# Loading chunk 0's K and Q in halves of heads, with another order of the opening, in a fused window-attention and maxout kernel

## The chip, the cores and the metric

The kernel runs on one core of a Trainium2 chip. The metric is the time of one execution in device microseconds (us). PE is the matrix engine (PEld its weight loads), DVE the vector engine, ACT the scalar engine, POOL the GpSimd engine; SP issues DMAs. Inputs and output are float32; the kernel works in bfloat16 on the chip and sums in float32.

## The reference

A sliding-window attention with four sink tokens (4 batches, 8 heads, 768 tokens, head size 64) feeds a feed-forward layer that takes the maximum of three products:

```python
    scores = scale * np.matmul(q, k.transpose(0, 1, 3, 2))
    keep = is_sink | in_window          # position < 4, or 0 <= i - j < 128
    scores = np.where(keep, scores, -1000000000.0)
    a = np.exp(scores - np.max(scores, axis=-1, keepdims=True))
    a = a / (np.sum(a, axis=-1, keepdims=True) + 1e-09)
    x = np.matmul(a, v)                 # then (B*S, H*D) = (3072, 512)
    h = np.maximum(np.maximum(x @ w1, x @ w2), x @ w3)   # 512 -> 768
    out = h @ w_out                                      # 768 -> 512
```

## The kernel before

The 3072 tokens are cut into 12 chunks of 256, three per batch. A window of 128 tokens needs at most the last half of the chunk ahead, and the four sinks come from the batch's first chunk. For each chunk (number `ci` in the calls) the work is this:

- `load` (line 90): K, Q and V of all 8 heads, 512 KB each, by DMA from SP's queue into one of two slots per kind. With `parts` a load can be cut into groups of heads. A `gate` is a tiny write by POOL into the slot, for which the DMA then waits; `after(wi)` (490) makes the gate wait for a piece of weights.
- `cast_qk` (102) and `cast_v` (108) cast to bfloat16, on the engine named in the call; a call takes half of the heads, or a quarter of V.
- `turn` (118) and `turn2` (140) turn half of K's or Q's heads by four PE transposes through PSUM and copy them to `kT` or `qT`. From chunk 4 on, a DMA does it (`turn_dma`, 157 and 162).
- `score` (287) makes the scores of a head pair, `premask` (269) puts an additive mask into PSUM ahead of it, `expo` (335) takes exponentials on ACT, `mask` (341) multiplies masks in on DVE for pairs without `premask`.
- `sink_k`, `sink_score` and `sink_v` (242, 349, 365) handle the sinks. `av_open` and `av` (381, 398) multiply with V on PE; DVE normalises by a reciprocal (403) and a product (406) into `x_sb`.
- `xpose` (419) turns x into `xT` for the feed-forward layer, by PE and a copy (420); from chunk 4 on a DMA does it.
- `ffn_h(ci, fp, wi)` (438): eight matmuls of 128x256 for columns 256 fp to 256 fp + 255 of weight matrix `wi` (0 to 2). For `wi` 0 ACT copies the result to `h_sb` (445); for 1 and 2 DVE takes the maximum with what stands there (449). So the two maxima of a group of columns read ACT's copy.
- `ffn_y` (459, copies at 461): the output product with `wo`, six matmuls of 128x512; `store` sends it out.

The weights come by DMA from POOL's queue (`load_w` 251, `load_wo` 257), cast on the way, in pieces of 256 or 512 columns. `masks_late` (213, 215) makes multiplicative masks on POOL; `masks_packed` (221 to 224) makes four more copies of them on ACT, for the packed scores of chunks 6 and 9 (`score_packed`). `warm` (180) issues products of zeros that fill PE's time at the start.

Nothing reorders the work: each engine runs its instructions in the order in which the calls stand in the program. PSUM has 8 banks, handed out in the order in which earlier tiles are given back in the program, so a call also waits for its bank's last reader. The opening, lines 507 to 709 before, is one flat list of calls, up to chunk 3's `xpose`. From line 715 a loop runs chunks 3 to 11 by fixed patterns.

Of the kernel before, what the change touches and what calls it, by code (L numbers as in the profile page):

```python
# [16 lines left out]
def kernel(  # L17
# [13 lines left out]
    nc = tc.nc  # L31
# [17 lines left out]
    with tc.manual_schedule():  # L49
# [26 lines left out]
        def load(ci, what="kqv", gate=None, part=None, parts=1):  # L76
            if ci >= NCH:
                return
            b, c = divmod(ci, CPB)
            t0 = c * 256  # L80
            for w in what:
                src = {"k": k, "q": q, "v": v}[w]
                if (ci, w) not in raws:
                    raws[ci, w] = raw.tile([128, H, 2, D], F32, tag=w + "_raw", name=w + "_raw")
                dst = raws[ci, w]
                if gate is not None:
                    gate(dst[0:1, 0, 0, 0:1])
                n = H // parts
                for g in range(parts) if part is None else (part,):
                    nc.sync.dma_start(  # L90
                        out=dst[:, n * g:n * g + n],
                        in_=src[b, n * g:n * g + n, t0:t0 + 256]
                            .rearrange("h (p i) d -> p h (i d)", i=2))

        def cast_qk(ci, w, g, eng):
            if ci >= NCH:
                return
            if (ci, w) not in bfs:
                bfs[ci, w] = raw.tile([128, NP, 2, 2, D], BF16, tag=w + "_bf", name=w + "_bf")
            x, y = bfs[ci, w], raws[ci, w]  # L100
            f = eng.copy if eng is nc.scalar else eng.tensor_copy
            f(x[:, 2 * g:2 * g + 2].rearrange("q p i a d -> q p a i d"),  # L102
              y[:, 4 * g:4 * g + 4].rearrange("q (p a) i d -> q p a i d", a=2))
# [409 lines left out]
        premask(0, (0,))  # L513
        warm(9)
        cast_qk(0, 'k', 0, nc.scalar)
        turn(0, 'k', 0, nc.vector)
        load(0, 'v')
        cast_qk(0, 'q', 0, nc.scalar)
        turn(0, 'q', 1, nc.vector)
        sink_init()  # L520
        warm(1)
        cast_qk(0, 'k', 1, nc.gpsimd)
        cast_v(0, 1, 0, nc.vector)
        turn(0, 'k', 1, nc.scalar)
        load(1, 'k')
        turn(0, 'q', 0, nc.scalar)
        cast_v(0, 0, 1, nc.vector)
        score(0, (2,))
        masks_late()
        premask(0, (1,))  # L530
        load_w(0, 512, 768)
        load_w(0, 0, 512)
        cast_v(0, 0, 0, nc.vector)
        load(1, 'q')
        score(0, (0,))
        sink_k(0)
        expo(0, 2)
        load_w(1, 512, 768)
        cast_qk(1, 'k', 0, nc.vector)
        expo(0, 0)  # L540
        premask(0, (3,))
        cast_v(0, 1, 1, nc.vector)
        cast_qk(1, 'q', 0, nc.gpsimd)
        score(0, (1,))
        premask(1, (1,))
        turn2(1, 'k', 0, nc.vector)
        cast_qk(1, 'k', 1, nc.scalar)
        score(0, (3,))
        expo(0, 1)
        cast_qk(1, 'q', 1, nc.gpsimd)  # L550
        load(1, 'v')
        turn2(1, 'k', 1, nc.scalar)
        expo(0, 3)
        av_open(0)
        av(0, 0)
        av(0, 1)
        sink_v(0)
        turn2(1, 'q', 0, nc.vector)
        load_w(1, 0, 512)
        turn2(1, 'q', 1, nc.scalar)  # L560
        av(0, 2)
        av(0, 3)
        cast_v(1, 1, 1, nc.vector)
        score(1, (0,))
        expo(1, 0)
        sink_score(1)
        cast_v(1, 0, 1, nc.gpsimd)
        score(1, (1,))
        cast_v(1, 1, 0, nc.gpsimd)
        load(2, 'q', gate=pool_gate)  # L570
        score(1, (2,))
        expo(1, 2)
        xpose(0, 1, nc.vector)
        xpose(0, 0, nc.vector)
        cast_v(1, 0, 0, nc.vector)
        premask(1, (3,))
        expo(1, 1)
        score(1, (3,))
        ffn_h(0, 2, 0)
        mask(1, 2)  # L580
        load(2, 'k', gate=after(0, 300))
        mask(1, 0)
        load_w(2, 512, 768)
        av_open(1)
        av(1, 2)
        av(1, 1)
        load_w(2, 0, 256)
        expo(1, 3)
        load(2, 'v', gate=after(1))
        av(1, 0)  # L590
        ffn_h(0, 1, 0)
        load(3, 'q', gate=after(0))
        av(1, 3)
        ffn_h(0, 0, 0)
        load_w(2, 256, 512)
        xpose(1, 1, nc.vector)
        xpose(1, 0, nc.scalar)
        ffn_h(0, 2, 1)
        cast_qk(2, 'q', 0, nc.gpsimd)
        load_wo(0, 3)  # L600
        ffn_h(1, 0, 0)
        ffn_h(1, 1, 0)
        load_wo(3, 6)
        ffn_h(1, 2, 0)
        load(3, 'k', gate=after(1))
# [5 lines left out]
        load(3, 'v', gate=after(2))  # L611
        cast_qk(2, 'k', 1, nc.scalar)
        cast_qk(2, 'k', 0, nc.gpsimd)
        cast_qk(2, 'q', 1, nc.vector)
        ffn_h(1, 2, 1)
        turn(2, 'q', 0, nc.scalar)
        ffn_h(1, 2, 2)
        turn(2, 'q', 1, nc.scalar)
        turn(2, 'k', 1, nc.vector)
        cast_v(2, 0, 1, nc.gpsimd)  # L620
        turn(2, 'k', 0, nc.vector)
        ffn_h(1, 0, 2)
        load(4, 'q')
        sink_score(2)
        score(2, (1,))
        load(4, 'k', gate=after(2))
        cast_v(2, 0, 0, nc.gpsimd)
        score(2, (2,))
        score(2, (3,))
        expo(2, 3)  # L630
        expo(2, 1)
        ffn_h(1, 1, 2)
        ffn_h(0, 0, 2)
        expo(2, 2)
        mask(2, 1)
        ffn_h(0, 1, 2)
        cast_v(2, 1, 1, nc.vector)
        cast_qk(3, 'q', 0, nc.gpsimd)
        cast_v(2, 1, 0, nc.vector)
        score(2, (0,))  # L640
        mask(2, 2)
        expo(2, 0)
        mask(2, 0)
        av_open(2)
        mask(2, 3)
        cast_qk(3, 'q', 1, nc.gpsimd)
        load(4, 'v', gate=pool_gate)
        ffn_y(1, 0)
        ffn_y(0, 0)
        cast_qk(3, 'k', 0, nc.scalar)  # L650
        av(2, 2)
        ffn_y(0, 1, nc.vector)
        av(2, 0)
        turn(3, 'q', 1, nc.scalar)
        turn(3, 'q', 0, nc.scalar)
        av(2, 3)
        av(2, 1)
        cast_qk(3, 'k', 1, nc.scalar)
        turn(3, 'k', 0, nc.scalar)
        cast_v(3, 1, 0, nc.vector)  # L660
        ffn_y(1, 1)
        cast_v(3, 1, 1, nc.gpsimd)
        turn(3, 'k', 1, nc.vector)
        xpose(2, 0, nc.scalar)
        xpose(2, 1, nc.vector)
        score(3, (0,))
        expo(3, 0)
        score(3, (3,))
        score(3, (1,))
        load(5, 'k')  # L670
        expo(3, 1)
        mask(3, 0)
        cast_v(3, 0, 0, nc.gpsimd)
        score(3, (2,))
        cast_v(3, 0, 1, nc.gpsimd)
        cast_qk(4, 'q', 1, nc.gpsimd)
        cast_qk(4, 'k', 1, nc.gpsimd)
        cast_qk(4, 'k', 0, nc.vector)
        ffn_h(2, 1, 0)
        expo(3, 2)  # L680
        expo(3, 3)
        ffn_h(2, 1, 1)
        cast_qk(4, 'q', 0, nc.gpsimd)
        mask(3, 1)
        mask(3, 3)
        mask(3, 2)
        ffn_h(2, 2, 0)
        ffn_h(2, 0, 0)
        av_open(3)
        turn_dma(4, 'k')  # L690
        ffn_h(2, 2, 1)
        turn_dma(4, 'q')
        av(3, 3)
        load(5, 'v', gate=after(0))
        ffn_h(2, 0, 2)
        av(3, 0)
        cast_v(4, 0, 1, nc.scalar)
        masks_packed()
# [12 lines left out]
        def sinks(n):
            if n % CPB == 1:
# [232 lines left out]
```

## Time and profile before

| what | us |
|---|---|
| median of 3 runs | 177.87 |
| runs | 177.29 to 178.0 |
| profiled execution | 177.2 |
| its span, first to last instruction | 175.4 |
| busy: PE / DVE / ACT / POOL | 168.9 / 123.5 / 88.8 / 66.9 |
| DMA read / written | 25.17 MB / 6.29 MB |

The profile is of one execution. A row of its timeline has the start and the length in us, the engine, the line, the operation and the tiles (out<-in); x4 means four instructions merged, and brackets hold the idle time before them with what ended it. Ends of matmuls are modelled, so a PE that is shown busy can hide short waits. In the chain of work that ended last, each piece is followed back to what released it. The granted clock of PE was 1.00 throughout.

### The profile page before, as it was taken

To read this page: it belongs to the slowest core of one execution; us is meant where nothing else is said; L and a number is where in the kernel's file an instruction comes from. 1 tells how busy PE (TensorE), PEld (TensorE's weight loads), DVE (VectorE), ACT (ScalarE), POOL (GpSimd) and SP (SyncE) were. 2 spreads that over 40 slices of the span, in tenths; PEclk is the share of its full clock that TensorE was granted. 3 is DMA by queue.
4 is the path that set the end of the run, shared out by engine and by line. 5 is a ranking of instruction groups with operands and counts; after the bars stand their busy time and mean duration, and the time that the engine had idled before them with its cause. 6 is when DMAs were issued, how large, how long until landed. Compare 5 with 4: busy or idle time off the path is not lost.

```text
span 175.4 us, 4631 instructions
## 1 busy us (share of the span) xinstructions
PE 168.9 (96%) x1872; PEld 127.1 (72%) x1872; DVE 123.5 (70%) x264; ACT 88.8 (51%) x173; POOL 66.9 (38%) x123
## 2 busy tenths in 40 slices
PE   6989999999999999999999999999999999999991
PEld 2446889856896697697796796796895895896870
DVE  3389828599698496895875975877775775976460
ACT  3398741586995823814716715715517617510211
POOL 6785335046480555734735328038246000000000
PEclk9999999999999999999999999999999999999999
DMA  4999999994999989899999999999999429223203
GB/s 134 291 289 205 215 259 254 216 278 124 297 168 237 107 214 238 168 294 150 214 305 162 260 278 149 274 247 142 274 271 125 149 51 398 95 54 129 120 2 120
DMA packets 69573, 34.90 MB, mean 199 GB/s; under 512 B 26544, under 2 KB 68016, under 8 KB 69552
## 3 DMA queue, kind: packets, MB, share of 16 engines
q1 hardware_dynamic: 64912, 31.33, 80.0%
q0 software_dynamic: 4496, 3.15, 11.8%
q8 instruction: 14, 0.23, 0.6%
q10 hardware_dynamic: 144, 0.13, 0.2%
q14 instruction: 7, 0.06, 0.1%
HBM read 25.17 MB, written 6.29 MB: 179 GB/s over the span
## 4 chain that ended last, share of the span: by engine, by line
PE 90%; DMA 4%; SPq 2%; POOL 1%; issue 0%; DVE 0%; ACT 0%; POOLq 0%
PE h_ps L438 54%; PE y_ps L459 18%; PE o L398 6%; PE st L287 6%; DMA q_raw<-in_q_dram 4%; SPq L90 2%; PE xt L419 1%; PE o L381 1%; PE pt L118 1%; PE sk L349 1%; PE st L307 1%; PE y_ps L469 1%; POOL q_bf L102 1%; PE st L269 0%; PE pt L140 0%
## 5 line engine op out<-in xcount | busy, mean ns | idle before, releaser
L438 PE MATMUL h_ps<-xT,w 128*128 128x256 bf16 x864 | 100.4, 273 | 0.0
L438 PEld LDWEIGHTS <-w 128*128 128x128 bf16 x864 | 82.2, 98 | 10.2 <-issue 0.5
L449 DVE TENSOR_TENSOR h_sb<-h_sb,h_ps 128x512 bf16<-128x512 bf16 (+1 forms) x74 | 49.2, 671 | 20.3 <-PE h_ps L438 19.1
L445 ACT CAST h_sb<-h_ps 128x512 bf16<-128x512 f32 x36 | 21.2, 590 | 42.9 <-PE h_ps L438 42.9
L335 ACT ACTIVATE e_sb<-st 128x512 bf16<-128x512 f32 (+1 forms) x80 | 40.2, 593 | 1.0 <-PE st L287 0.8
L108 POOL CAST vb<-v_raw 64x512 bf16<-64x512 f32 x38 | 27.4, 722 | 15.6 <-DMA v_raw<-in_v_dram 10.7
L459 PE MATMUL y_ps<-wo,h_sb 128*128 128x512 bf16 x138 | 32.2, 380 | 0.0
L341 DVE TENSOR_TENSOR e_sb<-e_sb,msk 128x1024 bf16<-128x1024 bf16 (+1 forms) x34 | 24.9, 765 | 3.5 <-ACT e_sb L335 3.3
L459 PEld LDWEIGHTS <-h_sb 128*128 128x128 bf16 x138 | 12.6, 98 | 14.8 <-issue 1.2
L406 DVE TENSOR_TENSOR x_sb<-o,rc 128x256 bf16<-128x256 f32 x48 | 20.4, 425 | 1.7
L102 POOL CAST k_bf<-k_raw 128x512 bf16<-128x512 f32 x17 | 10.3, 625 | 28.5 <-DMA k_raw<-in_k_dram 25.8
L102 POOL CAST q_bf<-q_raw 128x512 bf16<-128x512 f32 x21 | 13.3, 659 | 14.9 <-DMA q_raw<-in_q_dram 11.4
L461 DVE COPY y_sb<-y_ps 128x512 f32<-128x512 f32 x13 | 9.0, 690 | 10.9 <-PE y_ps L459 10.8
L398 PE MATMUL o<-vb,e_sb 128*128 128x65 bf16 x352 | 16.4, 193 | 0.0
L398 PEld LDWEIGHTS <-e_sb 128*128 128x128 bf16 x352 | 14.6, 97 | 2.3
L287 PE MATMUL st<-qT,kT 64*128 64x128 bf16 (+1 forms) x224 | 12.5, 237 | 0.5 <-ACT kT L125 0.5
L287 PEld LDWEIGHTS <-kT 64*128 64x128 bf16 x224 | 7.1, 94 | 6.0 <-issue 3.8
L355 ACT ACTIVATE e_sink<-sk 128x256 bf16<-128x256 f32 x8 | 3.1, 386 | 15.0 <-PE sk L349 10.5
L403 DVE RECIPROCAL rc<-o 128x4 f32<-128x4 f32 x48 | 8.4, 176 | 3.2 <-PE o L398 3.1
L318 ACT ACTIVATE e_sb<-st 128x512 bf16<-128x512 f32 x12 | 6.1, 613 | 4.7 <-PE st L307 4.7
L461 ACT COPY y_sb<-y_ps 128x512 f32<-128x512 f32 x10 | 5.9, 588 | 2.1 <-PE y_ps L459 1.6
L102 ACT CAST k_bf<-k_raw 128x512 bf16<-128x512 f32 x5 | 3.1, 627 | 6.7 <-DMA k_raw<-in_k_dram 6.7
(78 smaller groups left out, 87.6 us busy)
## 6 DMA issues: line engine op xcount, KB each, us to landing
k_raw<-in_k_dram SPq DMA_DIRECT2D x12, 512.0 KB, 5.7
q_raw<-in_q_dram SPq DMA_DIRECT2D x12, 512.0 KB, 6.8
v_raw<-in_v_dram SPq DMA_DIRECT2D x12, 512.0 KB, 8.1
out_dram<-y_sb SPq DMA_DIRECT2D x11, 512.0 KB, 4.1
w<-in_moe_w_dram POOLq DMA_DIRECT2D x5, 256.0 KB, 8.6
w<-in_moe_w_dram POOLq DMA_DIRECT2D x2, 512.0 KB, 9.8
wo<-in_moe_w_out_dram POOLq DMA_DIRECT2D x2, 384.0 KB, 9.7
kT<-k_bf SPq DMA_TRANSPOSE x16, 3.5
```

Of the source, the lines that this page charges most:

```text
L102: f(x[:, 2 * g:2 * g + 2].rearrange("q p i a d -> q p a i d"), y[:, 4 * g:4 * g + 4].rearrange("q (p a) i d -> q p a i d", a=2))
L108: (eng.copy if eng is nc.scalar else eng.tensor_copy)(vb[ci % RING][64 * i:64 * i + 64, n, :, 0:D], raws[ci, "v"][64 * n:64 * n + 64, :, i])
L287: nc.tensor.matmul(st[a][:, s:s + q1 - q0].rearrange("q n (i r) -> q n i r", i=2), lhsT=x[hp, n, p].rearrange("q i r -> q (i r)"), rhs=qc[ ...
L335: nc.scalar.activation(e[:, a, lo:], st[a][:, lo:], AF.Exp, scale=scale)
L341: (eng or nc.vector).tensor_mul(e[:, :, lo:], e[:, :, lo:], msk0 if lo else msk)
L398: nc.tensor.matmul(o[:, t, a], lhsT=weight(ci, p, a, s), rhs=vb[cv % RING][:, n, 2 * p + a], start=first, stop=True, skip_group_check=True)
L406: nc.vector.tensor_mul(xs[ci][:, :, p], o[:, :, :, 0:D], rc.unsqueeze(3).to_broadcast([128, 2, 2, D]))
L438: nc.tensor.matmul(hp[:, f].rearrange("q (i t r) -> q i t r", i=2, t=2), lhsT=w_sb[wi][:, ds, c0:c0 + 128], rhs=xTs[ci][:, :, ds].rearrang ...
L445: nc.scalar.copy(dst, hp)
L449: nc.vector.tensor_max(dst[:, x], dst[:, x], hp[:, x])
L459: nc.tensor.matmul(yp, lhsT=hs[ci][:, fb, t * 128:(t + 1) * 128], rhs=wo[:, fb], start=(fb == 0), stop=(fb == FB - 1))
L461: (nc.scalar.copy if eng is None else eng.tensor_copy)(ys[ci][:, t], yp)
```

## The change

K and Q of chunk 0 are loaded in two halves of heads each: K's first, Q's first, K's second, Q's second. The gate ahead of Q's load goes; chunk 1's K gets one. The rest of the list, up to chunk 3's `xpose`, holds the same work in another order, in part on other engines. The buffers and the loop behind the list stay as they are. The start of the diff:

```diff
-        load(0, 'k')
-        load(0, 'q', gate=pool_gate)
+        load(0, 'k', part=0, parts=2)
+        warm(2)
+        load(0, 'q', part=0, parts=2)
+        load(0, 'k', part=1, parts=2)
+        load(0, 'q', part=1, parts=2)
         masks()
...
```

**DVE in the opening.** The rows of DVE from the cast of chunk 0's second Q half (k_bf and q_bf are cast K and Q, vb is cast V, x_sb the attention's output). Before:

```order
L102 CAST q_bf<-q_raw 128x2x2x2x64
L125 COPY kT_69<-pt 128x2x256
L122 COPY qT_73<-pt 128x512
L108 CAST vb_77<-v_raw 64x8x64 x3
L102 CAST k_bf<-k_raw 128x2x2x2x64
L108 CAST vb_77<-v_raw 64x8x64
L147 COPY kT_70<-pt 128x2x256
L403 RECIPROCAL rc<-o 128x4
L406 TENSOR_TENSOR x_sb<-o,rc 128x2x128
```

Now, at the same place:

```order
L125 COPY kT_69<-pt 128x2x256
L102 CAST q_bf<-q_raw 128x2x2x2x64
L122 COPY qT_73<-pt 128x512
L108 CAST vb_77<-v_raw 64x8x64
L125 COPY kT_69<-pt 128x2x256
L108 CAST vb_77<-v_raw 64x8x64
L102 CAST k_bf<-k_raw 128x2x2x2x64
L108 CAST vb_77<-v_raw 64x8x64 x2
L147 COPY kT_70<-pt 128x2x256 x2
L403 RECIPROCAL rc<-o 128x4
L406 TENSOR_TENSOR x_sb<-o,rc 128x2x128
```

DVE now makes both of chunk 0's kT copies and both of chunk 1's before the first normalisation; ACT made one of each. Between the normalisations of chunk 0 and its two xT copies (L420), DVE now has two V casts of chunk 1 instead of one, the second from POOL.

**The first use of w2 on PE.** In the diff, the h products that follow chunk 1's `xpose`, without the lines between:

```diff
-        ffn_h(0, 2, 1)
-        ffn_h(1, 0, 0)
-        ffn_h(1, 1, 0)
-        ffn_h(1, 2, 0)
-        ffn_h(1, 0, 1)
-        ffn_h(1, 1, 1)
-        ffn_h(0, 0, 1)
-        ffn_h(0, 1, 1)
-        ffn_h(0, 2, 2)
+        ffn_h(0, 2, 1)
+        ffn_h(1, 2, 0)
+        ffn_h(1, 0, 0)
+        ffn_h(1, 1, 0)
+        ffn_h(0, 1, 1)
+        ffn_h(1, 0, 1)
+        ffn_h(1, 2, 2)
```

The first product with `wi` 2 was the ninth of them and is the seventh now. In both kernels it reads columns 512 to 767 of that matrix, which `load_w(2, 512, 768)` brings behind `load(2, 'k', gate=after(0, 300))`.

**ACT around the packed masks.** The rows of ACT from chunk 3's exponentials (e_sb<-st) to its xT copy. Before:

```order
L335 ACTIVATE e_sb<-st 128x384 x4
L445 CAST h_sb<-h_ps 128x512
L335 ACTIVATE e_sb<-st 128x384 x4
L445 CAST h_sb<-h_ps 128x512 x2
L108 CAST vb_77<-v_raw 64x8x64
L221 COPY mskp<-msk_101 128x2x384
L222 COPY mskp<-msk_101 128x2x128
L224 COPY mskp<-msk_101 128x2x256 x2
L420 COPY xT<-xt 128x512
```

Now:

```order
L335 ACTIVATE e_sb<-st 128x384 x6
L445 CAST h_sb<-h_ps 128x512
L335 ACTIVATE e_sb<-st 128x384 x2
L102 CAST k_bf<-k_raw 128x2x2x2x64
L221 COPY mskp<-msk_101 128x2x384
L222 COPY mskp<-msk_101 128x2x128
L224 COPY mskp<-msk_101 128x2x256 x2
L445 CAST h_sb<-h_ps 128x512 x2
L420 COPY xT<-xt 128x512
```

The four copies of packed masks stood behind all three h copies of chunk 2; they stand ahead of two of them now, (2,1,0) and (2,0,0). On DVE the maximum of `ffn_h(2, 1, 1)`, which reads the copy of (2,1,0), is followed by chunk 3's first normalisation (L403, L406), the maximum of (2,1,2), the other three normalisations and the two maxima of (2,0,2) and (2,0,1).

More of the change, by code (lines that the diff above doesn't have):

```diff
@@ L546 @@
[L546 to L552, printed above, removed]
+        sink_init()
+        premask(0, (0,))
+        turn(0, 'q', 1, nc.scalar)
+        turn(0, 'q', 0, nc.vector)
+        cast_v(0, 0, 1, nc.vector)
+        cast_qk(0, 'k', 1, nc.gpsimd)
+        turn(0, 'k', 1, nc.vector)
+        score(0, (1,))
+        masks_late()
+        cast_v(0, 0, 0, nc.vector)
@@ new lines @@
+        premask(0, (3,))
+        score(0, (0,))
+        cast_qk(1, 'k', 0, nc.vector)
+        premask(1, (1,))
+        expo(0, 1)
+        cast_v(0, 1, 1, nc.vector)
+        premask(0, (2,))
+        load_w(0, 512, 768)
+        expo(0, 0)
+        cast_qk(1, 'k', 1, nc.scalar)
+        score(0, (2,))
+        load_w(0, 0, 512)
+        score(0, (3,))
+        load(1, 'q')
+        load(1, 'v')
+        sink_k(0)
+        cast_v(0, 1, 0, nc.vector)
+        turn2(1, 'k', 0, nc.vector)
+        expo(0, 2)
@@ L573 @@
[L573 to L576, printed above, removed]
         expo(1, 1)
         score(1, (3,))
+        cast_v(1, 0, 0, nc.vector)
         ffn_h(0, 2, 0)
+        load(2, 'k', gate=after(0, 300))
+        load_w(2, 512, 768)
         mask(1, 2)
-        load(2, 'k', gate=after(0, 300))
+        av_open(1)
+        load_w(2, 0, 256)
         mask(1, 0)
-        load_w(2, 512, 768)
-        av_open(1)
+        expo(1, 3)
+        av(1, 1)
@@ L613 @@
[L613 to L627, printed above, removed]
+        ffn_h(1, 2, 2)
+        ffn_h(1, 2, 1)
@@ L628 @@
+        cast_qk(2, 'k', 1, nc.gpsimd)
+        turn(2, 'q', 0, nc.scalar)
+        ffn_h(0, 0, 1)
+        cast_qk(2, 'k', 0, nc.scalar)
+        ffn_h(0, 2, 2)
+        turn(2, 'q', 1, nc.vector)
+        ffn_h(1, 0, 2)
+        turn(2, 'k', 1, nc.vector)
+        turn(2, 'k', 0, nc.vector)
+        ffn_h(1, 1, 1)
         score(2, (2,))
         score(2, (3,))
+        cast_v(2, 1, 0, nc.gpsimd)
+        expo(2, 2)
+        cast_v(2, 0, 0, nc.gpsimd)
+        score(2, (1,))
+        sink_score(2)
@@ L630 @@
+        load(3, 'v', gate=after(2))
+        ffn_h(0, 0, 2)
         expo(2, 3)
         expo(2, 1)
+        ffn_h(0, 1, 2)
         ffn_h(1, 1, 2)
-        ffn_h(0, 0, 2)
-        expo(2, 2)
-        mask(2, 1)
[L636 to L642, printed above, removed]
+        score(2, (0,))
+        av_open(2)
+        expo(2, 0)
+        ffn_y(0, 0)
+        load(4, 'q')
@@ L650 @@
[L650 to L652 removed]
+        load(4, 'k', gate=after(2))
+        av(2, 1)
         av(2, 0)
+        turn(3, 'k', 0, nc.vector)
+        cast_v(3, 0, 1, nc.gpsimd)
         turn(3, 'q', 1, nc.scalar)
[L655 to L660, printed above, removed]
+        cast_qk(4, 'q', 0, nc.gpsimd)
         ffn_y(1, 1)
[L662 removed]
+        turn(3, 'q', 0, nc.vector)
@@ L663 @@
         turn(3, 'k', 1, nc.vector)
+        load(4, 'v')
         xpose(2, 0, nc.scalar)
```

167 lines of the change are left out of this document (76 added, 91 removed).

## The prediction

> **What bounds the kernel now.** I read the page first, then the chain of work that ended last in order of time, then the timeline of the opening by engine. The page's busy line, two of its 40-slice lines and the chain's shares:
>
> ```profile
> PE 168.9 (96%) x1872; PEld 127.1 (72%) x1872; DVE 123.5 (70%) x264; ACT 88.8 (51%) x173; POOL 66.9 (38%) x123
> PE   6989999999999999999999999999999999999991
> DMA  4999999994999989899999999999999429223203
> PE 90%; DMA 4%; SPq 2%; POOL 1%; issue 0%; DVE 0%; ACT 0%; POOLq 0%
> ```
>
> PE is busy for 96% of the span, and the DMA engines are full for the first nine slices (to 39.5 us) except in the first. The chain in order of time (start, us, what) says where the one hands over to the other:
>
> ```profile
> 4.92 7.32 DMA q_raw<-in_q_dram
> 13.60 0.40 PE pt L140 x4
> 16.84 1.00 PE h_ps L438 x8
> 21.51 8.74 PE h_ps L438 x80
> 44.76 0.86 PE st L287 x16
> 54.40 0.45 PE xt L419 x8
> 55.39 1.40 PE y_ps L459 x6
> 171.60 0.30 DVE y_sb L473
> ```
>
> Up to 13.6 us the chain hangs on the load of chunk 1's Q. From 13.60 to 171.60 it is PE without a break. So the change can only act in two ways: PE begins its unbroken stretch earlier or later with the same work done, or an order on another engine breaks the stretch. What PE loses there it never gets back. I have therefore followed the new order along the engines, with the durations of this execution, and compared four points: the first h product (16.84), the first of the ten products in a row (21.51), the first score of chunk 3 (44.76) and the turning of chunk 3's x (54.40).
>
> **The opening to 21.5 us.** The casts that follow the first loads, with the wait that ended before them:
>
> ```profile
> 5.04 0.62 ACT L102 CAST k_bf<-k_raw 128x512 bf16<-128x512 f32 x1 [2.80 <-DMA k_raw<-in_k_dram]
> 6.83 0.52 DVE L102 CAST q_bf<-q_raw 128x512 bf16<-128x512 f32 x1 [3.01 <-DMA q_raw<-in_q_dram]
> 8.64 1.76 DVE L108 CAST vb<-v_raw 64x512 bf16<-64x512 f32 x3 [0.34 <-DMA v_raw<-in_v_dram]
> 8.92 0.34 PE L287 MATMUL st<-qT,kT 64*128 64x256 bf16 x4 [0.46 <-ACT kT L125]
> ```
>
> Loads land 1.8 us apart (5.04, 6.83, 8.64), so halves should land 0.9 apart: K's first at 4.1, Q's first at 5.0, K's second at 5.9, Q's second still at 6.83. In the new order PE turns that last half first, so it gains little: cast to 7.4, both Q halves turned by 8.05, the copies done at 8.45, first score at 8.5 instead of 8.92. The filler (11 products, then 4, instead of 4, 9 and 1) ends before 7.4 in both. The gain of 0.4 us then runs into DVE:
>
> ```profile
> 10.45 0.43 DVE L102 CAST k_bf<-k_raw 128x512 bf16<-128x512 f32 x1
> 10.90 0.43 DVE L108 CAST vb<-v_raw 64x512 bf16<-64x512 f32 x1
> 11.47 0.42 DVE L147 COPY kT<-pt 128x512 bf16<-128x512 bf16 x1
> 12.26 0.18 DVE L403 RECIPROCAL rc<-o 128x4 f32<-128x4 f32 x1 [0.37 <-PE o L398]
> 12.82 0.17 DVE L403 RECIPROCAL rc<-o 128x4 f32<-128x4 f32 x1
> 13.37 0.28 DVE L368 CAST vs<-sv 128x130 bf16<-128x130 f32 x1
> 13.57 0.42 DVE L144 COPY qT<-pt 128x512 bf16<-128x512 bf16 x1
> 15.43 0.44 DVE L108 CAST vb<-v_raw 64x512 bf16<-64x512 f32 x1
> 15.90 0.76 DVE L420 COPY xT<-xt 128x512 bf16<-128x512 bf16 x2
> ```
>
> From the landing of chunk 1's K (10.42) to both copies of xT, DVE now has: the K cast 0.43, two V casts 0.87, two kT copies 0.8, four reciprocal-and-multiply pairs of 0.56 (12.26 to 12.82), qT 0.42, vs 0.28, two more V casts 0.87, xT 0.76. That is 6.7 us without a wait: 10.45 + 6.7 = 17.15. One kT copy came from ACT and one V cast from POOL. Before, xT ended at 16.66, with 0.6 us of waits on the way. So the first h product starts at about 17.2 instead of 16.84, and some of it is won back where PE waited for chunk 1's masks before (the av products after it). I carry **0.15 to 0.4 us late** to the point at 21.51. Bounds: 0.6 early (all waits of the old order gone) to 0.9 late (nothing won back, DVE slower beside POOL).
>
> **The third weight matrix, near 27 us.** Of the products that start at 21.51, one takes 8.74 / 80 x 8 = 0.874 us. The first product that reads w2 was the ninth from there: 21.51 + 8 x 0.874 = 28.5 us. Now it is the seventh: 21.51 + 6 x 0.874 = 26.75, plus the lateness above, 26.9 to 27.15. When do its columns 512 to 768 arrive? The issue on POOL, and the DMA table's row for the first of the two pieces (count, size, us from issue to landing):
>
> ```profile
> 19.03 1.49 POOL L251 DMA_DIRECT2D w<-in_moe_w_dram  x2
> w<-in_moe_w_dram POOLq DMA_DIRECT2D x1, 256.0 KB, 8.6
> ```
>
> 19.03 + 8.6 = 27.6 us. Its issue waits in both kernels for the landing of w0, ahead of it stand the same loads, and the DMA engines are full from 3 us on. So it can't come sooner by anything that PE does, and PE waits until 27.6: against the 26.75 of the old pace that is **+0.9 us**. The lateness of the opening disappears in this wait; if the opening were early, the wait would be longer by as much. Bounds: 0.3 (loads 0.6 earlier, rival D) to 0.9 + 1.0 = 1.9 (loads 1.0 later, rival A). From there to the first score of chunk 3 I find nothing that PE waits for: K and V of chunk 2 and all of wo are loaded in time as before, and the number of products between is the same.
>
> **The packed masks, 45 to 56 us.** This is the largest term. Before, ACT made them when it had nothing else to do:
>
> ```profile
> 45.09 1.66 ACT L335 ACTIVATE e_sb<-st 128x384 bf16<-128x384 f32 x4
> 46.72 0.59 ACT L445 CAST h_sb<-h_ps 128x512 bf16<-128x512 f32 x1
> 42.86 0.63 ACT L102 CAST k_bf<-k_raw 128x512 bf16<-128x512 f32 x1
> 50.59 0.83 ACT L221 COPY mskp<-msk 128x768 bf16<-128x768 bf16 x1
> 51.33 0.40 ACT L222 COPY mskp<-msk 128x256 bf16<-128x256 bf16 x1
> 51.64 1.14 ACT L224 COPY mskp<-msk 128x512 bf16<-128x512 bf16 x2
> 54.92 0.59 ACT L420 COPY xT<-xt 128x512 bf16<-128x512 bf16 x1 [2.15 <-issue]
> ```
>
> They took 50.59 to 52.78, 2.2 us, and 2.15 us of idle time followed. Now these four copies and the cast of chunk 4's K stand ahead of the two remaining h copies, (2,1,0) and (2,0,0). Counted from the first score of chunk 3 (44.76 before), ACT runs: first exponential at 0.33, six exponentials of 0.415 to 2.82, h copy to 3.41, two exponentials to 4.24, K cast to 4.87, masks to 7.06, h copy (2,1,0) to **7.65**. PE had that product ready at 4.3. Next in DVE's order is the maximum that reads this copy, and behind it, all of chunk 3's x:
>
> ```profile
> 51.67 0.68 DVE L449 TENSOR_TENSOR h_sb<-h_sb,h_ps 128x512 bf16<-128x512 bf16 x1
> 53.92 1.87 DVE L449 TENSOR_TENSOR h_sb<-h_sb,h_ps 128x512 bf16<-128x512 bf16 x3
> ```
>
> Maximum 0.68 to 8.33, one pair 0.56 to 8.9, maximum to 9.57, three pairs to 11.25, two maxima of 0.62 to 12.5. PE is done with its products at 54.40 - 44.76 = 9.64 and must wait for x until 11.25; then it turns x, makes two scores, and waits until 12.5 for the last maxima before the first y product. Before, that product began at 55.39 - 44.76 = 10.63. **+1.9 us.** Bounds: 0 if ACT reached the copy by 5.7, to 2.4 if DVE runs beside a busy POOL (three V casts took 1.76 above, 0.59 each, and the later one 0.44). Then the code is the old loop, PE-bound, and gives nothing back. DVE's idle time hides the maxima today; here that cover is gone, and x is what is late.
>
> **Sum.** The profiled execution took 177.2 us: 175.4 of span and 1.8 around it. 177.2 + 0.9 + 1.9 = 180.0. The median shown is 177.87, the runs go from 177.29 to 178.0, so this execution is at the fast edge; I leave the forecast at **180.0**, +1.2% on the median.
>
> **Rivals.**
>
> (A) Halves slow the whole stream. The issue of one load and the gap behind it took 1.88 - 1.38 = 0.5 us:
>
> ```profile
> 1.38 0.45 SPq L90 DMA_DIRECT2D q_raw<-in_q_dram  x1
> 1.88 1.35 SPq L90 DMA_DIRECT2D v_raw<-in_v_dram  x1
> ```
>
> If the two additional loads each hold the stream up by that, every weight lands 1.0 later: 181.0. Against it: whole loads land 1.8 us apart, so what a load costs beside its data lies under the data of the load ahead of it. A rule stands beside this rival. The Trainium skill, DMA: Bandwidth & Descriptors, section Anatomy of one DMA, gives each DMA (of the GpSimd kind) about 2.0 us fixed and bytes over 436 GB/s besides; its section Bandwidth advises at least 1 MiB each, which speaks against halves. If that fixed part stood in line, the estimate by the skill's figure would be 4 us for two more loads, and the sum 184. The trace doesn't bear that out: 1.8 us is all that a whole load takes of the stream.
>
> (B) w2 is in time (w2 lands by 26.7 or PE reaches it later for other reasons that cost nothing), only the masks count: 179.1.
>
> (C) The masks stay hidden, only w2 counts: 178.1. Against it: the sum of ACT's rows.
>
> (D) Not slower: the load stream moves forward. In two windows of the start (from:to, length, busy times of PE, PEld, DVE, ACT, POOL, then clock, DMA share, GB/s):
>
> ```profile
> 2.50:3.00 0.50, 0.50 (x2) 0.10 (x1) 0.39 (x3) 0.00 (x0) 0.44 (x3) 1.00 0.45 106
> 3.00:3.50 0.50, 0.08 (x1) 0.00 (x0) 0.43 (x4) 0.00 (x0) 0.44 (x5) 1.00 1.14 347
> ```
>
> If four short loads fill the 0.9 us before 3.0, which ran at about 100 instead of 290 to 347 GB/s, all landings come 0.6 us earlier; the chain before 13.6, which waits for a load, moves up by that, and w2 costs 0.3. The price is -0.6 + 0.3 + the masks' wait. It decides only if ACT is at that h copy 1.9 us sooner than worked out, when the end is 176.9.
>
> **How the numbers follow.** Forecast 0.55, A 0.10, B 0.12, C 0.12, D 0.06, and 0.05 for a further wait that I did not find (182 and more). 0.5% is 0.9 us, about what a measurement of this kernel can tell from no change. So faster is D, 0.06; C at 178.1 is within it, 0.12; the others are slower, 0.82. The range goes from 178.2, just above C, to 181.8, which is A with 0.8 for DVE's and the opening's upper bounds; about 0.8 lies inside.
>
> **What would show it.** In the profile of the changed kernel: PE idle, ended by a DMA of w, before the seventh product of the run, near 27.6 us; ACT's L221 to L224 straight behind a K cast, then L445; DVE idle some 2 us before an L449 that ACT's L445 releases; PE idle before L419 near 56 us, released by DVE. If DVE shows no idle time before that maximum, the largest term is wrong. If w lands clearly before 27 or after 28.5, the second is.

## The result, and the profile after

The changed kernel is slower: median 180.72 us (180.12 to 180.77) against 177.94 us (177.29 to 178.21) for the kernel before beside it, a ratio of 1.0154, 95% interval [1.0119, 1.0189]. Forecast: 180.0. Its profiled execution took 180.77 us with a span of 179.0, against 177.2 and 175.4. So the two profiles stand 3.6 us apart, the medians 2.8: the profile of before is at the low end of its times, the one of after at the high end.

The page's busy line, PE's 40 slices and the shares of the chain that ended last:

```profile
PE 168.6 (94%) x1861; PEld 127.1 (71%) x1873; DVE 126.4 (71%) x268; ACT 86.7 (48%) x169; POOL 68.9 (39%) x123
PE   7788998999997999999999999999999999999991
PE 67%; DMA 19%; ACT 4%; POOL 3%; DVE 3%; issue 1%; SPq 1%; POOLq 0%; DVEq 0%; ACTq 0%
```

PE has the same work (168.6 us busy against 168.9) in a longer span, and slices below 9 stand up to the thirteenth, 54 to 58 us. The chain of work in order of time (start, us, what) goes through other engines up to there:

```profile
14.07 5.25 DMA w<-in_moe_w_dram
51.46 0.72 ACT mskp L221
53.52 0.50 ACT h_sb L445
54.04 0.69 DVE h_sb L449
58.22 0.70 DVE h_sb L449
59.41 1.03 PE y_ps L459 x4
```

Before, it was PE without a break from 13.60. Now ACT's packed masks and a maximum on DVE lie on it at 51 to 59 us. The starts of five rows of PE in the two timelines say where the time went:

| point on PE | before | after | later by | new in this stretch |
|---|---|---|---|---|
| first h product (L438) | 16.80 | 17.76 | 0.96 | |
| run of h products behind the second `xpose` | 21.35 | 22.12 | 0.77 | 0.77 |
| first output product (L459) | 37.09 | 38.74 | 1.65 | 0.88 |
| first score of chunk 3 (L287 x16) | 44.69 | 46.87 | 2.18 | 0.53 |
| first output product of chunk 2 | 55.33 | 58.97 | 3.64 | 1.46 |

Behind the last point both spans have 120.0 us left. All of the loss lies in the opening list, and none of it comes back.

**The opening.** Casts behind the first loads in the timeline of after, and the first scores:

```profile
3.83 0.62 ACT L102 CAST k_bf<-k_raw 128x512 bf16<-128x512 f32 x1 [1.59 <-DMA k_raw<-in_k_dram]
4.73 0.62 ACT L102 CAST q_bf<-q_raw 128x512 bf16<-128x512 f32 x1 [0.28 <-DMA q_raw<-in_q_dram]
6.39 0.61 POOL L102 CAST k_bf<-k_raw 128x512 bf16<-128x512 f32 x1 [2.70 <-DMA k_raw<-in_k_dram]
7.26 0.73 DVE L102 CAST q_bf<-q_raw 128x512 bf16<-128x512 f32 x1 [0.96 <-DMA q_raw<-in_q_dram]
9.18 0.34 PE L287 MATMUL st<-qT,kT 64*128 64x256 bf16 x4 [0.29 <-DVE qT L122]
```

The first halves land 1.2 and 2.1 us ahead of the whole loads (5.04 and 6.83), the last one 0.4 behind whole Q. PE needs that one too, and scores at 9.18, not 8.92. DVE's rows ahead of xT, and the first h product:

```profile
12.46 0.74 DVE L147 COPY kT<-pt 128x512 bf16<-128x512 bf16 x2
15.96 0.86 DVE L108 CAST vb<-v_raw 64x512 bf16<-64x512 f32 x2
16.86 0.76 DVE L420 COPY xT<-xt 128x512 bf16<-128x512 bf16 x2
17.76 1.03 PE L438 MATMUL h_ps<-xT,w 128*128 128x256 bf16 x8 [0.37 <-DVE xT L420]
```

DVE makes both kT copies and both V casts and hands xT over at 17.62 instead of 16.66; the bracket names it.

**w2.** Its issue on POOL, the landing in the DMA table (us from issue), and the first product that reads it:

```profile
19.26 1.49 POOL L251 DMA_DIRECT2D w<-in_moe_w_dram  x2
w<-in_moe_w_dram POOLq DMA_DIRECT2D x1, 256.0 KB, 8.9
28.23 1.92 PE L438 MATMUL h_ps<-xT,w 128*128 128x256 bf16 x16 [0.71 <-DMA w<-in_moe_w_dram]
```

19.26 + 8.9 = 28.2, and PE waits 0.71 for it.

**A V cast.** DVE, POOL and PE from 38 to 42 us in after, then PE at the same place in before:

```profile
38.90 1.04 DVE L341 TENSOR_TENSOR e_sb<-e_sb,msk 128x1024 bf16<-128x1024 bf16 x1
41.11 0.72 DVE L108 CAST vb<-v_raw 64x512 bf16<-64x512 f32 x1
38.78 0.61 POOL L102 CAST k_bf<-k_raw 128x512 bf16<-128x512 f32 x1 [3.13 <-DMA k_raw<-in_k_dram]
40.47 1.09 POOL L102 CAST q_bf<-q_raw 128x512 bf16<-128x512 f32 x1 [1.07 <-DMA q_raw<-in_q_dram]
41.89 0.38 PE L398 MATMUL o<-vb,e_sb 128*128 128x65 bf16 x7 [0.35 <-POOL k_raw L490]
```

```profile
39.70 0.40 PE L398 MATMUL o<-vb,e_sb 128*128 128x65 bf16 x8
```

The last bracket names a gate on POOL, but the product reads vb, which DVE finishes at 41.83. From the first of these eight products (41.34) to the output products behind them (42.12) it takes 0.78 us, and 0.24 in before (39.70 to 39.94), so this wait is the whole 0.53 of that stretch. DVE's order there is new: the cast stands behind two mask products. Two of these rows of DVE are also longer than others of their kind, the mask 1.04 instead of 0.69 and the cast 0.72 instead of 0.43, each while a cast runs on POOL. In kernel 3 below the same two are long and the place takes 0.77; in kernels 1, 2, 5, 6, 11 and 12 one row ahead of the product is long and it takes 0.42 to 0.46.

**The masks.** ACT, DVE and PE from 50 to 59 us:

```profile
50.76 0.70 ACT L102 CAST k_bf<-k_raw 128x512 bf16<-128x512 f32 x1
51.27 0.91 ACT L221 COPY mskp<-msk 128x768 bf16<-128x768 bf16 x1
52.31 1.21 ACT L224 COPY mskp<-msk 128x512 bf16<-128x512 bf16 x2
53.35 0.66 ACT L445 CAST h_sb<-h_ps 128x512 bf16<-128x512 f32 x1
54.04 0.69 DVE L449 TENSOR_TENSOR h_sb<-h_sb,h_ps 128x512 bf16<-128x512 bf16 x1 [1.65 <-ACT h_sb L445]
57.58 0.56 PE L419 MATMUL xt<-ident,x_sb 128*128 128x128 bf16 x7 [0.93 <-DVE x_sb L406]
58.97 1.47 PE L459 MATMUL y_ps<-wo,h_sb 128*128 128x512 bf16 x5 [0.27 <-DVE h_sb L449]
```

This is the predicted order: cast, masks, then the h copy. DVE stands 1.65 us for that copy, PE 0.93 for x and 0.27 for the last maxima.

### The profile page after: what moved, and what is told of

The parts are those of the page before. It is cut to its first block, busy times and chain, and to the rows that moved or that the text cites. A ratio compares the mean times of both kernels' runs of the same rounds, so it can differ in the third digit from the quotient of the medians.

```text
span 179.0 us, 4627 instructions
## 1 busy us (share of the span) xinstructions
PE 168.6 (94%) x1861; PEld 127.1 (71%) x1873; DVE 126.4 (71%) x268; ACT 86.7 (48%) x169; POOL 68.9 (39%) x123
## 4 chain that ended last, share of the span: by engine, by line
PE 67%; DMA 19%; ACT 4%; POOL 3%; DVE 3%; issue 1%; SPq 1%; POOLq 0%; DVEq 0%; ACTq 0%
PE h_ps L438 40%; PE y_ps L459 15%; DMA q_raw<-in_q_dram 12%; PE o L398 5%; DMA k_raw<-in_k_dram 4%; PE st L287 3%; DMA w<-in_moe_w_dram 3%; DVE h_sb L449 1%; ACT e_sb L335 1%; POOL q_bf L102 1%; PE st L307 1%; SPq L90 1%; PE o L381 1%; PE y_ps L469 1%; DVE x_sb L406 1%
## 5 line engine op out<-in xcount | busy, mean ns | idle before, releaser
L438 PE MATMUL h_ps<-xT,w 128*128 128x256 bf16 x864 | 100.9, 273 | 1.1 <-DMA w<-in_moe_w_dram 0.7
L438 PEld LDWEIGHTS <-w 128*128 128x128 bf16 x864 | 82.0, 98 | 11.4 <-DMA w<-in_moe_w_dram 1.0
L108 POOL CAST vb<-v_raw 64x512 bf16<-64x512 f32 x39 | 29.7, 762 | 12.8 <-DMA v_raw<-in_v_dram 10.7
L459 PE MATMUL y_ps<-wo,h_sb 128*128 128x512 bf16 x126 | 31.5, 380 | 0.9 <-DVE h_sb L449 0.3
L341 DVE TENSOR_TENSOR e_sb<-e_sb,msk 128x1024 bf16<-128x1024 bf16 (+1 forms) x34 | 26.3, 797 | 2.8 <-ACT e_sb L335 2.7
L102 POOL CAST k_bf<-k_raw 128x512 bf16<-128x512 f32 x18 | 11.1, 639 | 43.1 <-issue 24.7
L459 PEld LDWEIGHTS <-h_sb 128*128 128x128 bf16 x138 | 12.5, 98 | 15.2 <-DVE h_sb L449 1.1
L406 DVE TENSOR_TENSOR x_sb<-o,rc 128x256 bf16<-128x256 f32 x48 | 20.4, 425 | 1.6
L461 DVE COPY y_sb<-y_ps 128x512 f32<-128x512 f32 x12 | 8.3, 692 | 11.4 <-PE y_ps L459 11.4
L102 POOL CAST q_bf<-q_raw 128x512 bf16<-128x512 f32 x19 | 11.8, 640 | 10.5 <-DMA q_raw<-in_q_dram 9.5
L287 PE MATMUL st<-qT,kT 64*128 64x128 bf16 (+1 forms) x224 | 12.3, 237 | 0.5 <-DVE qT L122 0.3
L287 PEld LDWEIGHTS <-kT 64*128 64x128 bf16 x224 | 7.4, 94 | 5.8 <-issue 4.5
L403 DVE RECIPROCAL rc<-o 128x4 f32<-128x4 f32 x48 | 8.4, 175 | 2.3 <-PE o L398 2.0
L461 ACT COPY y_sb<-y_ps 128x512 f32<-128x512 f32 x11 | 6.5, 587 | 3.7 <-PE y_ps L459 3.3
L180 PE MATMUL warm<-wz 128*128 128x512 bf16 x15 | 5.1, 503 | 1.2 <-DVE wz L169 1.2
```

The lines of the kernel that those rows point to most:

```text
L108: (eng.copy if eng is nc.scalar else eng.tensor_copy)(vb[ci % RING][64 * i:64 * i + 64, n, :, 0:D], raws[ci, "v"][64 * n:64 * n + 64, :, i])
L287: nc.tensor.matmul(st[a][:, s:s + q1 - q0].rearrange("q n (i r) -> q n i r", i=2), lhsT=x[hp, n, p].rearrange("q i r -> q (i r)"), rhs=qc[ ...
L341: (eng or nc.vector).tensor_mul(e[:, :, lo:], e[:, :, lo:], msk0 if lo else msk)
L406: nc.vector.tensor_mul(xs[ci][:, :, p], o[:, :, :, 0:D], rc.unsqueeze(3).to_broadcast([128, 2, 2, D]))
L438: nc.tensor.matmul(hp[:, f].rearrange("q (i t r) -> q i t r", i=2, t=2), lhsT=w_sb[wi][:, ds, c0:c0 + 128], rhs=xTs[ci][:, :, ds].rearrang ...
L459: nc.tensor.matmul(yp, lhsT=hs[ci][:, fb, t * 128:(t + 1) * 128], rhs=wo[:, fb], start=(fb == 0), stop=(fb == FB - 1))
```

## The experiments

The theory: the loss has separate places (the masks, w2's first use, the opening with the halves and DVE's additional work). The rivals: one place causes it all, or each only hides another. Ratios are to the kernel before, timed beside each kernel.

| kernel | median us | ratio [95%] | run of h products | first y product of chunk 2 |
|---|---|---|---|---|
| changed kernel | 180.72 | 1.0154 [1.0119, 1.0189] | 22.12 | 58.97 |
| 1 masks back | 178.45 | 1.0039 [1.0005, 1.0073] | 21.95 | 56.40 |
| 2 w2 later | 179.54 | 1.0098 [1.0069, 1.0127] | 22.04 | 57.68 |
| 3 whole loads | 180.56 | 1.0148 [1.0119, 1.0177] | 21.81 | 58.79 |
| 4 V cast first | 179.95 | 1.0108 [1.0077, 1.0140] | 22.59 | 58.48 |
| 5 masks, w2, whole loads | 177.76 | 1.0003 [0.9991, 1.0015] | 21.91 | 56.48 |
| 6 as 5, DVE's work less | 177.61 | 1.0003 [0.9986, 1.0021] | 21.38 | 56.03 |
| 7 before with halves | 177.94 | 1.0017 [1.0003, 1.0032] | 22.11 | 56.23 |
| 8 before with early masks | 178.06 | 1.0026 [1.0010, 1.0042] | 21.34 | 56.13 |
| 9 as 7, V with a gate | 177.85 | 1.0007 [0.9991, 1.0022] | 21.85 | 55.97 |
| 10 before with w2 seventh | 178.34 | 1.0022 [1.0003, 1.0040] | 21.51 | 56.56 |
| 11 masks and w2 back, halves kept | 178.46 | 1.0045 [1.0027, 1.0064] | 22.18 | 56.74 |
| 12 as 11, DVE's work less | 178.10 | 1.0040 [1.0021, 1.0060] | 21.69 | 55.91 |

The last two columns come from one profiled execution each. One and the same opening begins its run of h products at 21.95 to 22.59 (changed kernel, 1, 2, 4 and 11) or at 21.34 to 21.51 (before, 8 and 10), so a few tenths between two single profiles say little.

**1. Masks back.** The changed kernel with the four copies behind all h copies again:

```diff
-        masks_packed()
         cast_v(4, 0, 1, nc.gpsimd)
...
         ffn_h(2, 0, 1)
+        masks_packed()
```

> The changed kernel with the four copies of packed masks alone moved behind the h copies of (2,1,0) and (2,0,0). Theory (the copies hold up the maximum on DVE and with it chunk 3's x): the stretch from the first score of chunk 3 to the first y product of chunk 2 shrinks from 12.1 us to the 10.6 us of the kernel before, DVE no longer waits 1.65 us before a maximum, and the time falls by 1.4 to 1.5 us, to about 179.3. Rival (the K cast on ACT, the V casts on POOL or DVE's own order make x late): the stretch stays at 11.5 us or more and the time within 0.5 us of the changed kernel.

DVE at the same maximum, and PE, in its timeline:

```profile
51.49 0.68 DVE L449 TENSOR_TENSOR h_sb<-h_sb,h_ps 128x512 bf16<-128x512 bf16 x1
55.20 0.61 PE L419 MATMUL xt<-ident,x_sb 128*128 128x128 bf16 x8
56.40 1.47 PE L459 MATMUL y_ps<-wo,h_sb 128*128 128x512 bf16 x5
```

No brackets: DVE does not wait for ACT, PE does not wait for x. From the first score of chunk 3 (45.64) to the last row it takes 10.76 us; before 10.64, after 12.10. The masks account for 1.34 of the 1.46 in that stretch. The time fell by 2.3 us, more than the 1.4 to 1.5 expected: the w2 wait is missing in this execution as well (178.13 us), and the six times fall into two groups, 178.03 to 178.13 and 178.78 to 179.44.

**2. w2 later.** The seventh product moved to ninth place:

```diff
-        ffn_h(1, 2, 2)
         ffn_h(1, 2, 1)
...
         ffn_h(0, 0, 1)
+        ffn_h(1, 2, 2)
```

> The changed kernel with the first product that reads w2 moved from the seventh to the ninth place. Theory (PE waits for w2's landing at 28.2 us): that wait of 0.7 us goes and the time falls by 0.7 us, to about 180.0. Rival (PE would only wait at the next place, for the K of chunk 2 or for the maxima on DVE): the first score of chunk 3 stays at 46.9 us and the time is that of the changed kernel.

PE's run of h products in its timeline:

```profile
22.04 6.28 PE L438 MATMUL h_ps<-xT,w 128*128 128x256 bf16 x56
28.37 1.80 PE L438 MATMUL h_ps<-xT,w 128*128 128x256 bf16 x15
```

Seven products run in one piece and the eighth follows at 28.37. w2 landed at 19.17 + 9.1 = 28.3, even later than in the profile above, and nothing waits. From 22.04 to the first output product (37.78) it is 15.74 us, exactly as before; after it was 16.62. The term is 0.88 us where w2 lands late. The median fell by 1.2 us instead of the 0.7 expected; no run shows where the rest lies.

**3. Whole loads.**

```diff
-        load(0, 'k', part=0, parts=2)
+        load(0, 'k')
         warm(2)
-        load(0, 'q', part=0, parts=2)
-        load(0, 'k', part=1, parts=2)
-        load(0, 'q', part=1, parts=2)
+        load(0, 'q', gate=pool_gate)
```

> The changed kernel with K and Q of chunk 0 loaded whole again, in the new order of everything else. Theory (halves make all later loads land 0.4 us later, as the landings of chunk 0's Q at 7.25 instead of 6.8 and of chunk 1's Q at 12.66 instead of 12.25 say): those landings go back, w2 lands near 27.7, and the time falls by 0.4 to 0.6 us, to about 180.2. Rival (the halves bring PE its first work earlier and the new order needs them): the first h product starts after 17.8 us and the time is the same or up to 0.5 us more.

The run of h products in its timeline:

```profile
21.81 5.40 PE L438 MATMUL h_ps<-xT,w 128*128 128x256 bf16 x48
28.07 1.92 PE L438 MATMUL h_ps<-xT,w 128*128 128x256 bf16 x16 [0.85 <-DMA w<-in_moe_w_dram]
```

The landings went back (K at 4.91, Q at 6.78) and the opening is 0.31 us earlier, but the first product with w2 starts only 0.16 earlier (28.07 instead of 28.23), after a wait of 0.85 instead of 0.71. Time 1.0148 against 1.0154. Half of the gain ahead of the wait for a landing is eaten by the wait: on the time the rival was right (though the first h product starts at 17.45, not after 17.8), and this edit could not measure the halves while that wait was there.

**4. V cast first.** One product with a mask behind the V cast that PE waits for:

```diff
-        mask(2, 3)
         cast_v(2, 1, 1, nc.vector)
...
         cast_v(2, 0, 1, nc.vector)
+        mask(2, 3)
```

> The changed kernel with the mask of (2,3) on DVE moved behind the two V casts of chunk 2. Theory (the first av product of chunk 2 waits 0.55 us for the V cast that stands behind two masks): that wait goes, the time falls by 0.5 us, to about 180.2. Rival (the wait only moves to the second av product, which reads the mask that is later now, or PE gets ahead and waits for x of chunk 3 as long as before): no change within 0.2 us.

PE two microseconds on, in its timeline:

```profile
43.41 0.42 PE L398 MATMUL o<-vb,e_sb 128*128 128x65 bf16 x8 [0.30 <-DVE e_sb L341]
```

A miss: the wait at the first product is gone, but PE now waits at the last of the four, for the mask of (2,0), which is DVE's last there (42.65 to 43.35) and not the mask that was moved. From the first output product to chunk 3's first score it takes 8.07 us against 8.13. This fits DVE as a whole being late there, not the one cast. The lower median can't be put down to the edit: its profile has no w2 wait, and that differs between executions of one kernel.

**5 and 6. All back, then DVE relieved.** Kernel 5 has the edits of 1, 2 and 3 together. Kernel 6 adds:

```diff
-        turn2(1, 'k', 1, nc.vector)
+        turn2(1, 'k', 1, nc.scalar)
...
-        cast_v(1, 0, 1, nc.vector)
+        cast_v(1, 0, 1, nc.gpsimd)
```

> The changed kernel with three of its parts put back: whole loads of chunk 0's K and Q, the first product with w2 behind two more products with w1 (ninth instead of seventh), and the packed masks behind the h copies. Theory (the three are separate terms of the loss): what is left of the 3.6 us of span is the opening order (0.46 us late at the run of h products, as with whole loads alone) and the waits of DVE and PE around chunk 2's first products (0.2 to 0.4), so the span is about 176.0 to 176.3 and the median 0.4% above the kernel before. Rival (the terms hide one another, and another wait takes their place): the span stays at 176.9 or more, 0.8% above or more.

> As the run with three parts put back, and one copy of chunk 1's kT goes back to ACT and one V cast of chunk 1 back to POOL. Theory (the additional 0.85 us of DVE's work ahead of xT is what makes the first h product late): first h product at 16.8 to 17.0 instead of about 17.4, span 0.4 us shorter than the run with three parts put back, within 0.3% of the kernel before. Rival (the waits for DMAs and the order of the products set the opening, or POOL's cast slows DVE as much as it saves): first h product no earlier, same time.

The first h product in 5, then in 6:

```profile
17.55 1.03 PE L438 MATMUL h_ps<-xT,w 128*128 128x256 bf16 x8 [0.37 <-DVE xT L420]
```

```profile
17.02 1.03 PE L438 MATMUL h_ps<-xT,w 128*128 128x256 bf16 x8
```

With three parts back the loss is gone: 1.0003. The theory had left 0.4%; the measured rest is below 0.15%, and the profiled execution (178.38 us) was the longest of its 12. So with masks, w2 and halves back the whole loss is gone, and the remaining new order by itself is worth nothing that the times resolve. The three are not worth as much elsewhere: added one at a time to the kernel before (8, 10 and 7 below) they cost 0.26, 0.22 and 0.17%, 0.65% together, against 1.51% in the new order. In the profiles, kernel 6's first h product is 0.53 earlier and the wait for xT gone, as the theory says; in the times 5 and 6 can't be told apart.

**7 and 9. The kernel before with halves.** The four half loads of the change in place of the two whole ones; kernel 9 also has `load(0, 'v', gate=pool_gate)`.

> The kernel before with one edit: K and Q of chunk 0 loaded in four halves in the changed kernel's order (the gate ahead of Q's load goes with it); the order of all other calls stays. Theory (the halves themselves slow the stream of loads): Q's second half lands 0.4 to 0.5 us later than whole Q did (7.26 against 6.8), all loads behind it 0.4 us later, first h product 0.3 to 0.5 us later, and the time 0.2 to 0.3% above. Rival (the lateness came from the order of the other work, not from the halves): landings and time as before, or earlier by the 0.9 us by which the first halves come sooner.

> The kernel before with K and Q of chunk 0 in halves, and V's load of chunk 0 held back by a gate until POOL has made its first masks (about 3.7 instead of 2.9 us), so that V is issued behind all four halves' transfers. Theory (the halves land late because bytes of the loads behind them move among theirs: up to 7.0 us the DMAs moved as much as before): Q's second half lands at about 7.0 instead of 7.6, the run of h products starts 0.4 to 0.6 us earlier than with ungated halves (22.11). Rival (the pieces themselves cost time, whatever stands behind): Q's second half at 7.5 or later, and V and all loads behind it later still, the run of h products at 22.1 or later.

The last half's cast and the first h product in 7, then the issue of V and that cast in 9:

```profile
7.62 0.87 DVE L102 CAST q_bf<-q_raw 128x512 bf16<-128x512 f32 x1 [3.85 <-DMA q_raw<-in_q_dram]
17.69 1.03 PE L438 MATMUL h_ps<-xT,w 128*128 128x256 bf16 x8
```

```profile
2.96 0.45 SPq L90 DMA_DIRECT2D v_raw<-in_v_dram  x1
7.21 0.74 DVE L102 CAST q_bf<-q_raw 128x512 bf16<-128x512 f32 x1 [3.41 <-DMA q_raw<-in_q_dram]
```

In the old order halves alone make the first h product 0.89 late in the profile (17.69 against 16.80), and the time 0.17% longer: more than expected in the profile, a little less in the time. Kernel 9 failed as an experiment: POOL reached the gate at 2.84, V was issued at 2.96 instead of 2.90, and nothing was held back. It stands as a second measurement of kernel 7: the same loads, a last half that lands 0.4 us sooner, a time 0.07% above. Why halves land later stays open.

**8. The kernel before with early masks.** `masks_packed()` ahead of the h copies (2,2,0) and (2,0,0).

> The kernel before with one edit: the four copies of packed masks stand on ACT ahead of the h copies (2,2,0) and (2,0,0) instead of behind them. Theory (the place of the masks by itself makes chunk 3's x late): masks from about 48.7 to 51.0, the next h copy done at about 51.6 instead of 49, DVE's maxima and normalisations 1.5 to 2 us later, x late by about 0.8, first output product of chunk 2 at 56.1 to 56.4 instead of 55.3, time 0.4 to 0.6% above. Rival (the masks cost only together with the other order of the maxima in the changed kernel): no wait of PE for x, same time.

ACT, DVE and PE in its timeline:

```profile
48.68 0.87 ACT L221 COPY mskp<-msk 128x768 bf16<-128x768 bf16 x1
50.74 1.11 ACT L445 CAST h_sb<-h_ps 128x512 bf16<-128x512 f32 x2
51.41 0.69 DVE L449 TENSOR_TENSOR h_sb<-h_sb,h_ps 128x512 bf16<-128x512 bf16 x1 [0.83 <-PE o L398]
54.94 0.56 PE L419 MATMUL xt<-ident,x_sb 128*128 128x128 bf16 x7 [0.50 <-DVE x_sb L406]
56.13 1.46 PE L459 MATMUL y_ps<-wo,h_sb 128*128 128x512 bf16 x5
```

The place of the masks alone makes x late (0.50) and the output product 0.80 late, in the expected bounds; the time, 0.26% longer, is below the expected 0.4 to 0.6%. (The bracket names PE, but the maximum starts just after ACT's first copy.) In the changed kernel the term is larger: DVE waits 1.65 instead of 0.83. That chunk 4's K cast (0.70) stands ahead of the masks there too fits this, but was not tried by itself.

**10. The kernel before with w2 seventh.** `ffn_h(0, 2, 2)` two places earlier.

> The kernel before with one edit: the first product with w2 is the seventh instead of the ninth from the start of the run of h products. Theory (its place alone makes PE wait for the landing): PE reaches it at 21.35 + 6 x 0.89 = 26.7; with the landings 7.5 to 9.1 us behind an issue at about 19.0 that is a wait of 0 to 1.4 us, on the average 0.6 to 0.9, and a time 0.3 to 0.5% above. Rival (w2's issue comes sooner when PE is early, or the wait is won back before the first output product): no wait, same time.

Its seventh product:

```profile
27.64 3.67 PE L438 MATMUL h_ps<-xT,w 128*128 128x256 bf16 x32 [0.72 <-DMA w<-in_moe_w_dram]
```

The same wait as in the changed kernel, and 16.64 us from the run of h products to the first output product instead of 15.74: 0.90 in this execution, 0.22% in the times, a little below what was expected. The landing comes 7.4 to 9.1 us after the issue from one profile to another, so some executions pay and others don't: of the five profiles with w2 seventh, the changed kernel, 3 and 10 wait (8.9, 9.1 and 8.4), 1 and 4 don't (7.5 and 7.4).

**11 and 12. Halves kept, the rest back.** 11 has the edits of 1 and 2; 12 those and the two of kernel 6.

> The changed kernel, halves kept, with only the packed masks and the first product with w2 put back. With the run that also loads whole (0.03% above the kernel before, 0.15% below to 0.1% above at its ends) it tells what the halves cost in the changed order. Theory (the halves land Q's second half 0.3 to 0.5 us later and the opening hands that on): 0.2 to 0.3% above the kernel before, run of h products at 22.0. Rival (the changed order absorbs the late half, as loading whole alone changed the time by only 0.06%): no more than 0.1% above.

> As the other run of this pair, halves kept, and besides one copy of chunk 1's kT on ACT and one V cast of chunk 1 on POOL, as in the kernel before. This is the changed kernel with all three found losses taken out, so the place where halves could win. Theory (DVE's additional 0.85 us ahead of xT sets the opening also with halves): first h product at 17.2 to 17.4 instead of 17.6 to 17.8, 0.2 us less than the other run. Rival (with halves the late landing of Q's second half sets the opening): no earlier, same time as the other run. Neither gives a time below the kernel before.

The first h product in 11, then in 12:

```profile
17.82 1.03 PE L438 MATMUL h_ps<-xT,w 128*128 128x256 bf16 x8 [0.37 <-DVE xT L420]
```

```profile
17.33 1.03 PE L438 MATMUL h_ps<-xT,w 128*128 128x256 bf16 x8
```

11 and 5 differ by the halves alone: 1.0045 / 1.0003 = 1.0042, with the half-widths 0.19% and 0.12% combined [1.0020, 1.0064]. So in the changed order halves cost about 0.75 us, more than the 0.2 to 0.3% expected; the rival, that the new order absorbs them, is out. In the old order they cost 0.17 and 0.07% (7 and 9). Where the 0.75 us lies isn't shown: the profiled executions of 11 and 5 took 178.52 and 178.38 us, and that of 5 was no typical one. DVE's relief shows in the profile again (0.49 us) and again not in the ratio (1.0040), though the medians point its way. Neither beats the kernel before, and no version here does.

## Why the prediction was right, and where it was not

**The direction and the largest cause held.** Putting masks, w2 and halves back together leaves nothing of the loss. Undone alone they give 1.15, 0.56 and 0.06%, added alone to the kernel before 0.26, 0.22 and 0.17%: what each is worth depends on the waits around it. The forecast was 0.7 us short. It was counted up from the profiled execution (177.2, at the low end of the times); between the two profiles the loss is 3.6 us, not 2.8, with 0.75 more in the opening and at w2, 0.53 more in a wait that was not foreseen and 0.44 less at the masks. That these misses partly cancel, and that the two medians lie 2.8 apart like the forecast's two terms, is luck.

**The opening, 0.15 to 0.4: measured 0.77.** "Halves should land 0.9 apart ... Q's second half still at 6.83" failed. The first two did, 0.3 early (3.83, 4.73); the second halves came at 6.39 and 7.26. In the seven profiles with halves where its cast shows the landing, Q's last half is there at 7.19 to 7.74, in the six with whole loads whole Q at 6.78 to 7.09. The DVE sum was right: from chunk 1's K cast (10.95) to the end of xT (17.62) it took 6.67 without a gap, against 6.7 (the K cast took 0.70 instead of 0.43, the other rows a little less). Its start was 0.5 late: that K landed at 10.85 (3.45 + 7.4), before at 10.4 (3.28 + 7.1), and DVE was busy up to 10.86. PE won back 0.19 behind it. Kernel 3 parts the 0.77, by single profiles: 0.46 stays with whole loads (21.81 against 21.35), 0.31 comes with the halves.

**w2, "it can't come sooner", +0.9: right in size, wrong in part of its ground.** The stretch lost 0.88, and kernel 3 shows an earlier opening lengthening the wait, 0.14 of 0.31. But I let the opening's lateness vanish in it, against a landing at 27.6; it came at 28.2 (issue 0.23 later, transfer 0.3 longer), so opening and w2 together cost 1.65 instead of 0.9. And w0, for which the issue was to wait, had landed by 18.03; the gate copy itself then took 1.28 us (last section).

**"From there to the first score of chunk 3 I find nothing that PE waits for" is the step that failed outright.** 0.53 us went there. I had counted products and loads, and not followed DVE's order of masks and V casts around 41 us. PE waited for a V cast behind two masks, and two of DVE's rows ran 0.3 us longer than others of their kind while POOL cast beside them. Experiment 4, which only moved the wait to the last mask, fits DVE as a whole being late there.

**The masks, +1.9: measured 1.46, of which 1.34 by experiment 1.** The mechanism was right row by row. From the first score of chunk 3, ACT's h copy ended at 54.01 - 46.87 = 7.14, not 7.65: chunk 4's K cast began 0.35 sooner. x came at 10.71 instead of 11.25, the output product at 12.10 instead of 12.5.

**The rivals.** A, halves slow the stream by 1.0, has about half its price: chunk 1's Q lands at 12.7 to 13.2 with halves, at 12.2 to 12.6 with whole loads. The estimate of 4 us, worked out from the fixed part that the Trainium skill, DMA: Bandwidth & Descriptors, section Anatomy of one DMA, gives a DMA of the GpSimd kind, does not come out for these loads in SP's stream, though halves do cost. D is out: from 2.5 to 3.0 us the DMAs did move 331 GB/s instead of 106, but the loads that PE needs last came no sooner. B and C each drop a term that the experiments showed.

**What stays open:** why halves land later and cost more in the new order than in the old, and DVE's additional 0.85 us ahead of xT, which moves the first h product by 0.5 in two pairs of profiles and by nothing that the times resolve.

## What to carry to other kernels

When an order is rewritten, follow the engines that the busiest one waits for (here DVE and ACT) row by row through the whole rewritten part: work that fills idle time at one place can lie on the path a few rows further up. A gain ahead of a landing that does not move with it is eaten by the wait, so take that wait away before measuring the gain. Cutting a load in parts brings the first part sooner but can bring the last one later, and helps only if the first part's consumers can do without the last.

## What the runs showed of the hardware

**A copy of one element on POOL waited for DVE's mask products.** POOL's gate copy (it reads one element of w from SBUF) and DVE's L341 (two SBUF inputs) in after, then in before:

```profile
18.03 1.28 POOL L490 CAST k_raw<-w 1x1 f32<-1x1 bf16 x1 [2.52 <-DMA w<-in_moe_w_dram]
17.98 1.28 DVE L341 TENSOR_TENSOR e_sb<-e_sb,msk 128x1024 bf16<-128x1024 bf16 x2
```

```profile
18.91 0.18 POOL L490 CAST k_raw<-w 1x1 f32<-1x1 bf16 x1 [3.32 <-DMA w<-in_moe_w_dram]
17.17 1.29 DVE L341 TENSOR_TENSOR e_sb<-e_sb,msk 128x1024 bf16<-128x1024 bf16 x2
```

In after the copy ends with the masks, at 19.3; in before the masks were over at 18.46 and it took 0.18. In kernels 7 and 9 it took 0.40 and 0.50 and ended just after the first of the two masks. Over all fourteen profiles it took 0.18 in the three where the masks were over (before, 8 and 10) and 0.40 to 1.50 in the others. The Trainium skill, SBUF — State Buffer, section SBUF: two separate sides, says that the pair of ports that DVE and GpSimd share is locked for a whole instruction, and names DVE operations with two SBUF inputs against a GpSimd operation that reads SBUF; these rows agree, and in after the copy was held through two such instructions. That w2 would have been in time without this was not tried.

**The landing of one piece of weights varied by 1.7 us** (7.4 to 9.1 us after its issue, 256 KB, profiles of nearly the same program), and with it whether PE waited at all. With halves it was 7.4 to 7.6 in six of eight profiles (8.9 and 9.1 in the changed kernel and 2), with whole loads 8.4 to 9.1 in all six; why is not known.
